# A top-k attention with a highway layer behind it: layer rows turned by DMA, one reduce for maximum and threshold, and a new order of evacuations

## The chip, the cores and the metric

The kernel runs on one core of a Trainium2 chip. The metric is the device time of one execution in microseconds. Before the change the median of three runs is 821.52 us.

## The reference, cut to what matters

Eight batch items, eight heads, 576 positions, 64 dimensions a head. Each query keeps its 32 largest scores; the result of the attention goes through a highway layer of width 512.

```python
scores = scale * np.matmul(q, k.transpose(0, 1, 3, 2))         # (8, 8, 576, 576)
kth = np.partition(scores, -32, axis=-1)[..., -32:-31]
scores = np.where(scores >= kth, scores, -1000000000.0)
attn = np.exp(scores - scores.max(-1, keepdims=True))
attn = attn / (attn.sum(-1, keepdims=True) + 1e-09)
x = np.matmul(attn, v)               # heads side by side: (4608, 512)
H = np.maximum(x @ w_h, 0.0)
T = 1.0 / (1.0 + np.exp(-(x @ w_t + b_t)))
out = T * H + (1.0 - T) * x
```

## The kernel before

**Tiling.** The 576 positions of an item are four blocks of 128 queries and a rest of 64. A unit is 128 query rows by 576 keys: one head of a full block, or two heads of the rest. Two units make a pair; an item has 18 pairs (16 of full blocks, then two of last rows), the whole kernel 144. The order is written out by hand: `step(i)` issues the instructions of several pairs in different stages, and each engine takes its own in that order. `finish` holds the last pair and the tail. A branch at the end recomputes everything if a count says that the selection was not certain; it is not taken here.

**One step.** TensorE computes the scores of pair i+2 in fp32 into PSUM (`scores`, lines 293 and 302; for last rows lines 310 and 319, where 64x64 quarters of the array are used). Two such score tiles exist, so those of pair i+2 need the place of pair i. VectorE takes the eight largest of each of six segments of a row (line 337), and from these `refine` works out a threshold near rank 24 (lines 351 to 367). `row_max` (line 372) reduces the candidates to the row's maximum. ScalarE copies the scores to SBUF (line 332), counts and marks those above the threshold (`mask_count`, line 381), and takes the exponential (line 400). TensorE adds the marks to the scores in PSUM (line 394), so that the eight largest of the rest (`below`, line 404) hold the wanted rank. `hits`, `pick_a` (GpSimd, line 420) and `pick_b` (line 423) pick it by the count. A pair later ScalarE (line 427) and GpSimd (line 438) mark the kept scores, VectorE multiplies or takes the minimum (`keep_min`, `keep_mul`, lines 434 and 444), and a DMA on SyncE's queue turns the kept rows (line 465). Three pairs later TensorE multiplies with V (`values`, line 478), whose 65th column is one, so that the sum comes along. ScalarE copies four heads of sums at a time from `pso` (line 492), that is every other step. `spare` (line 262) issues matmuls whose result nobody reads.

**Layer.** When a block of 128 rows has all heads, `ffn_pieces` makes `norm` (two small VectorE operations on the sums, lines 541 and 542, the scaling on GpSimd, line 547) and three pieces: `xt` (four transposes on TensorE, line 560, evacuated by ScalarE, line 564), `hh` and `tt` (projections, evacuated at lines 575 and 597). A step takes one piece from `layers`; its matmuls stand behind the scores of pair i+2, its evacuation is put in `late` and issued early in the next step. The rest of the layer's arithmetic is on GpSimd, in `pool_work`, and an accumulating DMA on GpSimd's queue (line 658).

**Next item.** `loads_kq` and `loads_v` bring K, Q and V. `prep_piece` turns K and Q on TensorE (line 239) and ScalarE evacuates them (line 240; line 251 to 253 for the last rows, in one piece). `prep_filler` takes such a piece in the middle of a step, beside whatever piece of a layer the step has. `todo_kq` is filled at an item's first step, `to_prep` at its seventh.

Of the kernel before, what the change touches and what calls it, by code (L numbers as in the profile page):

```python
# [10 lines left out]
ALU = mybir.AluOpType  # L11
# [6 lines left out]
J = 4  # L18
# [8 lines left out]
def kernel(  # L27
# [70 lines left out]
    wall = consts.tile([P, NU, NPK], FP32)  # L98
    fac = consts.tile([P, 4], FP32)
    nc.vector.memset(fac[:, 0:2], -scale)  # L100
    nc.vector.memset(fac[:, 2:4], -BIGK * (1.0 - 2.0**-24))
    tk = consts.tile([P, NG + 1, 4], FP32)
    be = consts.tile([P, NG + 1, 4], FP32)
# [7 lines left out]
    nc.vector.memset(tk[:, 0, 2:4], 0.0)  # L111
    nc.vector.memset(tk[:, NG, 0:2], 0.0)

    def top(u):
        return tk[:, u // 2, u % 2 : u % 2 + 1]

    def kth(u):
        return tk[:, u // 2 + 1, 2 + u % 2 : 3 + u % 2]

    def tb(u):  # L120
        return be[:, u // 2, u % 2 : u % 2 + 1]

    def eb(u):
        return be[:, u // 2 + 1, 2 + u % 2 : 3 + u % 2]

    NM = 4
# [20 lines left out]
    kds = []  # L147
    for i in range(2):
        kd = consts.tile([P, NP, P], FP32, name=f"kd{i}")
        nc.gpsimd.memset(kd[:], 0.0)  # L150
        kds.append(kd)

# [19 lines left out]
    def loads_v(b, vb):  # L172
# [11 lines left out]
        return [partial(head, h) for h in range(H)] + [partial(ends, o) for o in (0, P2)]  # L184
# [40 lines left out]

    def prep_piece(stage, prep, hp, part, ps=None, eng=None):
        kT, qT, kd = prep
# [8 lines left out]
        if part != 2:  # L236
# [3 lines left out]
            return lambda: copy(dst[:, hp, c0 * P : c1 * P], ps[:, c0 * P : c1 * P])  # L240
        for i, src in enumerate((kin, qin)):
            for h in range(NP):
# [7 lines left out]
        def evac():  # L250
            nc.scalar.copy(kd[0:D, :, 0:rem], view[0:D, 0, :, :])
            copy(kd[D:P, :, rem : 2 * rem], view[D:P, 0, :, :])
            nc.scalar.copy(qT[:, :, MAIN:S], view[:, 1, :, :])
# [17 lines left out]
    def prep_alloc(kd):  # L271
        kT = kqpool.tile([P, NP, MAIN], FP32, name="kT")
        qT = kqpool.tile([P, NP, S], FP32, name="qT")
        return kT, qT, kd
# [5 lines left out]
    def scores(pair, prep):  # L280
        kT, qT, kd = prep
# [23 lines left out]
        else:  # L305
            for (mo, ro), hh in zip(((0, RA), (MB, RB)), heads2):
                hp = hh[0] // 2
                for n0 in range(0, MAIN, 256):
                    for r in (0, D):
                        nc.tensor.matmul(  # L310
                            ps[r : r + rem, mo + n0 : mo + n0 + 256],
                            qT[r : r + D, hp, qs : qs + rem],
                            kT[r : r + D, hp, n0 : n0 + 256],
                            start=(n0 == 0),
                            stop=True,
                            skip_group_check=True,
                        )
                for r in (0, D):
                    nc.tensor.matmul(  # L319
                        ps[r : r + rem, ro : ro + rem],  # L320
                        qT[r : r + D, hp, qs : qs + rem],
                        kd[r : r + D, hp, r : r + rem],
                        start=(mo == 0),
                        stop=True,
# [17 lines left out]
    def refine(g, cand):  # L342
        u0, u1 = pairs[g][0], pairs[g][1] + 1
        en = ends[g % NE]
        runs = cand[:].rearrange("p s (k t) r -> p (s k) t r", t=2)
        one, two = runs[:, :, 0, :], runs[:, :, 1, ::-1]
# [3 lines left out]
        mid = cpool.tile([P, 2, 8], FP32, name="mid")  # L350
        nc.vector.tensor_tensor(high[:].rearrange("p (k r) -> p k r", r=8), one, two, ALU.max)  # L351
        yield
        nc.vector.tensor_tensor(low[:].rearrange("p (k r) -> p k r", r=8), one, two, ALU.min)
# [734 lines left out]
```

## Time and profile before

| | |
|---|---|
| median of 3 runs | 821.52 us (821.15 to 821.84) |
| profiled execution | 822.81 us, span 821.2 us |
| TensorE matmul, weight load | 714.2 us (87%), 517.6 us (63%) |
| VectorE | 784.9 us (96%) |
| ScalarE | 772.7 us (94%) |
| GpSimd | 556.1 us (68%) |
| mean DMA rate | 112 GB/s |

PE is TensorE's matmuls and PEld its weight loads, DVE is VectorE, ACT ScalarE, POOL GpSimd, SP SyncE. In a group of instructions the columns are the line, the engine, the operation, output and inputs, shapes and count, then the busy time in us and the mean of one in ns, and the idle time of the engine before them with what ended it. In a view of stretches the columns are the stretch and its length, the busy time of PE, PEld, DVE, ACT and POOL with instruction counts, TensorE's granted clock, the DMA share and the rate. A line of the timeline is start, duration, engine, line, operation, and in brackets the idle time before it. An fp32 matmul shows as two records.

### The profile page before, as it was taken

What the parts mean: (1) busy time and instruction counts of PE and PEld (TensorE: products, weight loads), DVE (VectorE), ACT (ScalarE), POOL (GpSimd) and SP (SyncE); (2) the same over time, 40 slices, a digit from 0 to 9 for tenths busy, and PEclk for the clock granted to TensorE, in tenths of its full rate; (3) what the DMA queues carried; (4) which work ended last, traced back from release to release, by engine and by line L of the source; (5) the groups of instructions that cost most, each with busy time, mean ns of one, the idle gap of its engine ahead of it and who ended that gap; (6) DMA issues with size and microseconds to landing.
All of it is one profiled execution on the core that took longest, in us unless ns stands there. A gap on an engine that the chain in (4) does not pass through costs nothing.

```text
span 821.2 us, 21236 instructions
## 1 busy us (share of the span) xinstructions
PE 714.2 (87%) x6687; PEld 517.6 (63%) x6687; DVE 784.9 (96%) x4162; ACT 772.7 (94%) x1438; POOL 556.1 (68%) x703
## 2 busy tenths in 40 slices
PE   7888988898889988889898898888988898888884
PEld 5666666666666666666666666666666666666552
DVE  6999999999999999999999999999999999999985
ACT  5999999999999999999999999999999999999983
POOL 2666777776677776777667776777667767666550
PEclk9999999999999999999999999999999999999998
DMA  6698878885568655775567765777556865444462
GB/s 120 84 137 140 109 105 129 140 118 84 107 126 142 108 91 110 131 137 108 83 121 132 137 104 72 133 139 131 92 94 129 142 113 97 92 88 72 103 90 74
DMA packets 323145, 91.61 MB, mean 112 GB/s; under 512 B 312144, under 2 KB 315216, under 8 KB 323024
## 3 DMA queue, kind: packets, MB, share of 16 engines
q1 hardware_dynamic: 272688, 74.76, 46.3%
q0 software_dynamic: 48656, 14.95, 18.5%
q8 instruction: 55, 0.90, 0.5%
q10 hardware_dynamic: 1680, 0.46, 0.3%
q14 instruction: 66, 0.54, 0.2%
HBM read 31.72 MB, written 9.44 MB: 50 GB/s over the span
## 4 chain that ended last, share of the span: by engine, by line
DVE 43%; ACT 39%; PE 13%; issue 2%; DMA 1%; SPq 0%; DVEq 0%; ACTq 0%
DVE cand L337 16%; DVE wall L404 12%; ACT m L381 11%; ACT e L400 8%; ACT sc L332 7%; ACT r L427 5%; PE xs L310 4%; PE pso L262 3%; DVE ep L434 3%; DVE ep L444 2%; ACT kT L240 2%; PE xs L293 1%; ACT xs L492 1%; ACT qT L240 1%; DVE en L358 1%
## 5 line engine op out<-in xcount | busy, mean ns | idle before, releaser
L337 DVE MAX8 cand<-xs 128x8 f32<-128x96 f32 x1728 | 297.4, 249 | 13.9 <-PE xs L319 9.4
L262 PE MATMUL pso<-cst,ident_b 128*128 128x252 bf16 x1935 | 256.5, 272 | 38.8 <-ACT xs L492 36.7
L438 POOL TENSOR_SCALAR ro<-sc,tk 128x576 bf16<-128x576 f32 x136 | 234.8, 1726 | 0.0
L262 PEld LDWEIGHTS <-ident_b 128*128 128x128 bf16 x1935 | 183.4, 98 | 77.8 <-issue 45.9
L400 ACT ACTIVATE e<-sc,be 128x576 bf16<-128x576 f32 x288 | 228.6, 794 | 0.0
L404 DVE MAX8 wall<-xs 128x8 f32<-128x576 f32 x288 | 204.3, 751 | 4.2 <-PE xs L394 3.6
L293 PE MATMUL xs<-kT,qT 64*128 64x256 f32 x1024 | 145.6, 400 | 35.2 <-DVE high L351 28.8
L332 ACT COPY sc<-xs 128x1152 f32<-128x1152 f32 x144 | 162.1, 1126 | 1.5 <-DVE cand L337 1.3
L293 PEld LDWEIGHTS xs<-kT,qT 64*128 64x128 f32 x1024 | 93.6, 186 | 64.7 <-issue 32.4
L381 ACT ACTIVATE m<-xs,wall 128x576 int8<-128x576 f32 x144 | 108.5, 754 | 13.1 <-DVE wall L367 10.7
L420 POOL TENSOR_TENSOR hit<-hit,wall 128x18 f32<-128x18 f32 x143 | 32.1, 225 | 128.4 <-DVE hit L410 119.1
L394 PE MATMUL xs<-m,ident_b 128*128 128x512 bf16 (+1 forms) x576 | 104.2, 285 | 11.9 <-ACT m L381 9.2
L381 ACT ACTIVATE m<-sc,wall 128x576 int8<-128x576 f32 x144 | 113.0, 784 | 0.0
L427 ACT ACTIVATE r<-sc,be 128x576 bf16<-128x576 f32 x143 | 111.4, 779 | 0.0
L375 POOL TENSOR_TENSOR be<-tk,fac 128x4 f32<-128x4 f32 x144 | 28.9, 201 | 93.4 <-DVE ep L444 51.8
L478 PEld LDWEIGHTS <-et 128*128 128x128 bf16 (+1 forms) x1600 | 68.6, 100 | 21.0 <-issue 3.5
L478 PE MATMUL pso<-vb,et 128*128 128x65 bf16 (+1 forms) x1600 | 74.6, 194 | 1.7 <-DMA et<-ep 1.6
L394 PEld LDWEIGHTS <-ident_b 128*128 128x128 bf16 x576 | 50.7, 97 | 39.7 <-issue 18.3
L302 PEld LDWEIGHTS xs<-kd,qT 128*128 128x128 f32 x256 | 38.1, 188 | 42.5 <-issue 42.1
L434 DVE TENSOR_TENSOR ep<-e,r 128x576 bf16<-128x576 bf16 x143 | 64.6, 452 | 0.1
L302 PE MATMUL xs<-kd,qT 128*128 128x128 f32 x256 | 62.5, 326 | 0.0
L444 DVE TENSOR_TENSOR ep<-e,ro 128x576 bf16<-128x576 bf16 x136 | 61.4, 452 | 0.0
(130 smaller groups left out, 1107.7 us busy)
## 6 DMA issues: line engine op xcount, KB each, us to landing
kin<-in_k_dram SPq DMA_DIRECT2D x64, 128.0 KB, 2.9
qin<-in_q_dram SPq DMA_DIRECT2D x62, 128.0 KB, 3.0
out_dram<-s SPq DMA_DIRECT2D x30, 256.0 KB, 2.5
s<-h POOLq DMA_DIRECT2D x29, 256.0 KB, 4.1
vb<-in_v_dram POOLq DMA_DIRECT2D x80, 64.0 KB, 3.2
et<-ep SPq DMA_TRANSPOSE x286, 2.7
kin<-in_k_dram SPq DMA_DIRECT2D x16, 64.0 KB, 2.4
qin<-in_q_dram SPq DMA_DIRECT2D x14, 64.0 KB, 2.5
```

The lines of the kernel that those rows point to most:

```text
L262: nc.tensor.matmul(po["t"][:, 4 * DE : BANK], ident_b[:], cst[:, 0 : BANK - 4 * DE], start=True, stop=True, skip_group_check=True,)
L293: nc.tensor.matmul(ps[:, mo + n0 : mo + n0 + 256], qT[r : r + D, hp, qs : qs + P], kT[r : r + D, hp, n0 : n0 + 256], start=(n0 == 0), stop ...
L302: nc.tensor.matmul(ends, qT[:, hp, qs : qs + P], kd[:, hp, :], start=True, stop=True)
L332: nc.scalar.copy(sc[:], both)
L337: nc.vector.max(cand[:, s, :], sc[:, s * SEG : (s + 1) * SEG])
L381: nc.scalar.activation(m1[:].bitcast(I8)[:, 1 : 2 * S : 2], ps, AF.Sign, bias=wall[:, u, 0:1], scale=ABOVE, accum_out=csum[:, u : u + 1],)
L394: nc.tensor.matmul(ps[:, s0:s1], ident_b[:], m1[:, s0:s1], start=False, stop=True, skip_group_check=True)
L400: nc.scalar.activation(e[:], sc, AF.Exp, bias=tb(u), scale=scale)
L404: nc.vector.max(wall[:, u, 1:NPK], ps)
L427: nc.scalar.activation(r[:], sc, AF.Relu, bias=eb(u), scale=BIGK)
L438: nc.gpsimd.tensor_scalar(r[:], sc, kth(u), None, ALU.is_ge)
L478: nc.tensor.matmul(pso[r0 : r0 + ql, col : col + DE], ets[s][:, c, gi * P2 : gi * P2 + ql], vb[:, h, vc, :], start=(c == 0), stop=(c == nc ...
```

## The change

- **Row maximum with threshold.** The four candidate tiles become constants with eight segment slots, of which two are filled with a very small number. `refine` writes its eight middle values into column 1 of the candidates, beside the segments' maxima in column 0, and one reduce gives the row maximum and the threshold. `row_max` goes; maxima, thresholds and picked ranks live together in `wall`.
- **Order on VectorE.** `pick_b` comes two operations earlier; the first kept row is computed between the middle values and the reduce.
- **Normaliser.** V's extra column is 2, and each head's product with V begins with an fp32 matmul of a single row that adds 2e-9, so that the reciprocal is taken directly and line 541 goes.
- **Layer rows by DMA.** For all blocks but the last three, `xt` is replaced by a cast to bf16 (a DMA on GpSimd's queue) and, two steps later, a DMA transpose on SyncE's queue; at most two such turns are under way.
- **One evacuated piece a step.** From the second item on, a step takes a piece of a layer or one of the next item's K and Q, in turn; the middle of a step takes another only where the count of pieces left asks for it. The last rows' piece is split in two (7 for K, 8 for Q).
- **Loads.** K and Q of the next item are requested two pairs sooner, their pieces become due five steps sooner; V of items after the first comes in four column loads instead of eight by head.
- **Last rows' queries as diagonal blocks.** Q of the last rows is kept in `qd` with zeros beside it, as K already was in `kd`, and the scores use the whole array with one matmul where there were two on quarters.

```diff
+    TOP, THR, KTH = 0, 1, NPK + 1
+    wall = consts.tile([P, NU + 2, NPK + 2], FP32)
...
-        nc.gpsimd.memset(vb[:, :, :, D:DE], 1.0)
+        nc.gpsimd.memset(vb[:, :, :, D:DE], 2.0)
...
+    tiny = consts.tile([1, DE], FP32)
+    nc.vector.memset(tiny[:], 0.0)
+    nc.vector.memset(tiny[:, D:DE], 2.0e-9)
+    row1 = consts.tile([1, P], FP32)
+    nc.vector.memset(row1[:], 1.0)
...
+        def column(j):
+            nc.gpsimd.dma_start(
+                vb[:, :, j, 0:D],
+                v[b, :, 0 : J * P, :].rearrange("h (p j) d -> p h j d", j=J)[:, :, j, :],
+            )
...
-            nc.scalar.copy(kd[0:D, :, 0:rem], view[0:D, 0, :, :])
-            copy(kd[D:P, :, rem : 2 * rem], view[D:P, 0, :, :])
-            nc.scalar.copy(qT[:, :, MAIN:S], view[:, 1, :, :])
+            if 0 in which:
+                nc.scalar.copy(kd[0:D, :, 0:rem], view[0:D, 0, :, :])
+                copy(kd[D:P, :, rem : 2 * rem], view[D:P, 0, :, :])
+            if 1 in which:
+                nc.scalar.copy(qd[0:D, :, 0:rem], view[0:D, 1, :, :])
+                copy(qd[D:P, :, rem : 2 * rem], view[D:P, 1, :, :])
...
-                    for r in (0, D):
-                        nc.tensor.matmul(
-                            ps[r : r + rem, mo + n0 : mo + n0 + 256],
-                            qT[r : r + D, hp, qs : qs + rem],
-                            kT[r : r + D, hp, n0 : n0 + 256],
...
+                    nc.tensor.matmul(
+                        ps[:, mo + n0 : mo + n0 + 256],
+                        qd[:, hp, :],
+                        kT[:, hp, n0 : n0 + 256],
...
                 for r in (0, D):
                     nc.tensor.matmul(
-                        ps[r : r + rem, ro : ro + rem],
-                        qT[r : r + D, hp, qs : qs + rem],
-                        kd[r : r + D, hp, r : r + rem],
+                        ps[:, ro : ro + rem],
+                        qd[:, hp, :],
+                        kd[:, hp, r : r + rem],
...
         nc.vector.scalar_tensor_tensor(
-            out=mid[:], in0=en[:, 1, :, 0:8], scalar=-1.0, in1=en[:, 0, :, 0:8], op0=ALU.mult, op1=ALU.min
+            out=cand[:, :, :, 1], in0=en[:, 1, :, 0:8], scalar=-1.0, in1=en[:, 0, :, 0:8], op0=ALU.mult, op1=ALU.min
         )
         yield
-        nc.vector.tensor_reduce(wall[:, u0:u1, 0], mid[:], mybir.AxisListType.X, ALU.max)
+        nc.vector.tensor_reduce(
+            wall[:, u0:u1, TOP : THR + 1],
+            cand[:, :, :, 0:2].rearrange("p s r k -> p s k r"),
+            mybir.AxisListType.X,
+            ALU.max,
+        )
...
-    def row_max(g):
-        nc.vector.tensor_reduce(tk[:, g, 0:2], st[g]["cand"][:, :, :, 0], mybir.AxisListType.X, ALU.max)
...
+                nc.tensor.matmul(
+                    pso[r0 : r0 + ql, col : col + DE], row1[:, 0:ql], tiny[:], start=True, stop=False
+                )
...
-            nc.vector.tensor_scalar(rinv[:, 0:nh], xs3[:, :, D], 1e-9, 2.0, ALU.add, ALU.mult)
-            nc.vector.reciprocal(rinv[:, 0:nh], rinv[:, 0:nh])
+            nc.vector.reciprocal(rinv[:, 0:nh], xs3[:, :, D])
...
-                ready.extend([xt, hh, tt])
+                if by_dma:
+                    casts.append(cast)
+                else:
+                    ready.extend([xt, hh, tt])
...
+        def cast():
+            xb = xpool.tile([P, dm], BF16, name="xb")
+            nc.gpsimd.dma_start(xb[:, 0:w], st["x"][:, 0:w])
+            return partial(turn, xb)
+
+        def turn(xb):
+            st["xT"] = fpool.tile([P, n_g, P], BF16, name="xT")
+            nc.sync.dma_start_transpose(st["xT"][:, 0:ng, :], xb[:, 0:w])
+            flying.append(b)
+            ready.extend([hh, tt])
...
+        if i == 3 or nb < B and i >= (nb - 2) * SPB + 16 > 16 - 1 and not to_prep:
+            stages[nb] = stage_tiles()
+            todo_kq.extend(loads_kq(nb, *stages[nb]))
...
-        ev = prep_filler()
+        ev = prep_filler() if to_prep and (i <= SPB or (len(to_prep) > 15 - k_in or len(layers) > 2) and i % 2) else None
...
-        if layers:
+        if layers and (last_steps or i <= SPB or kind[0] or not to_prep):
+            kind[0] = False
             late.append(layers.pop(0)())
+        elif i > SPB:
+            kind[0] = True
+            piece = prep_filler()
+            if piece:
+                late.append(piece)
...
         for _ in range(5):
             next(ra, None)
-        if nxt:
-            row_max(i + 1)
-        next(ra, None)
         if live:
             pick_b(pr, hit)
+        next(ra, None)
+        masked(0)
         for _ in ra:
             pass
...
+        last = masked(1)
...
+        while turns and turns[0][0] <= i and len(flying) < 2:
+            turns.pop(0)[1]()
```

More of the change, by code (lines that the diff above doesn't have):

```diff
@@ L182, in ends @@
             )
-        return [partial(head, h) for h in range(H)] + [partial(ends, o) for o in (0, P2)]
+        def column(j):
[3 more added lines that the diff above has]
+            )
+        mains = [partial(column, j) for j in range(J)] if b else [partial(head, h) for h in range(H)]
+        return mains + [partial(ends, o) for o in (0, P2)]
     def stage_tiles():
@@ L344, in refine @@
         en = ends[g % NE]
-        runs = cand[:].rearrange("p s (k t) r -> p (s k) t r", t=2)
-        one, two = runs[:, :, 0, :], runs[:, :, 1, ::-1]
+        one = cand[:, :, 0:NSEG:2, :]
+        two = cand[:, :, 1:NSEG:2, ::-1]
         high = cpool.tile([P, 2 * HALF], FP32, name="high")
@@ L384, in mask_count @@
             AF.Sign,
-            bias=wall[:, u, 0:1],
+            bias=wall[:, u, THR : THR + 1],
             scale=ABOVE,
@@ L731 @@
     late = []
+    kind = [False]
     def masks_of(g):
```

141 lines of the change are left out of this document (75 added, 66 removed).

## The prediction

> **What bounds the kernel now.** I read first the busy shares, then one period of the kernel (the 18 steps of one batch item) and some single steps in the view of stretches, then the groups by line, and last the timeline of single steps.
>
> ```profile
> PE 714.2 (87%) x6687; PEld 517.6 (63%) x6687; DVE 784.9 (96%) x4162; ACT 772.7 (94%) x1438; POOL 556.1 (68%) x703
> ```
>
> ```profile
> core 0: us, PE busy (x) PEld busy (x) DVE busy (x) ACT busy (x) POOL busy (x), PEclk, DMA share, GB/s
> 293.49:392.09 98.60, 87.80 (x827) 63.71 (x828) 96.31 (x515) 96.04 (x180) 71.06 (x89) 1.00 0.66 116
> ```
>
> ```profile
> 299.25:304.48 5.23, 4.77 (x42) 3.15 (x42) 5.23 (x28) 4.61 (x9) 3.91 (x4) 1.00 0.46 72
> 352.42:358.13 5.71, 4.67 (x47) 3.33 (x47) 5.32 (x29) 5.62 (x13) 4.52 (x8) 1.00 0.80 139
> 358.13:363.89 5.76, 5.17 (x51) 3.70 (x52) 5.33 (x28) 5.76 (x12) 3.90 (x4) 1.00 0.90 128
> 385.59:392.09 6.50, 5.81 (x60) 4.05 (x59) 5.61 (x32) 6.50 (x14) 5.24 (x7) 1.00 0.68 118
> ```
>
> The first rows show two engines full at once: a period of 98.60 us holds 96.31 of DVE and 96.04 of ACT. The steps show that they take turns. In the first step DVE never rests (5.23 of 5.23) and ACT has 0.62 us over. In the next two ACT has 13 and 12 instructions instead of 9, because a piece of a layer and a piece of the next item's K or Q are both evacuated in that step; DVE idles 0.39 and 0.43 us there. The last one, where the last rows' pairs begin, has both and loses 0.89 us on DVE. So a period is DVE's work plus some 2.3 us in which DVE waits for an overloaded ACT, or for PE at the last rows. Relief on DVE alone would soon run into ACT, and the change relieves both. PE is not far behind, and what the change puts on it is my main doubt.
>
> **DVE: the row maximum and the sum's small operation.**
>
> ```profile
> L372 DVE TENSOR_REDUCE tk<-cand 128x2 f32<-128x12 f32 x144 | 22.3, 155 | 0.0
> L337 DVE MAX8 cand<-xs 128x8 f32<-128x96 f32 x1728 | 297.4, 249 | 13.9 <-PE xs L319 9.4 <-PE xs L302 4.4
> L404 DVE MAX8 wall<-xs 128x8 f32<-128x576 f32 x288 | 204.3, 751 | 4.2 <-PE xs L394 3.6 <-PE pso L478 0.2
> L541 DVE TENSOR_SCALAR rinv<-xs 128x8 f32<-128x8 f32 (+1 forms) x38 | 6.3, 165 | 0.0
> ```
>
> ```profile
> 407.20 0.16 DVE L372 TENSOR_REDUCE tk<-cand 128x2 f32<-128x12 f32 x1
> 407.31 0.17 DVE L363 SCALAR_TENSOR_TENSOR mid<-en 128x16 f32<-128x16 f32 x1
> ```
>
> ```profile
> 424.29 0.17 DVE L541 TENSOR_SCALAR rinv<-xs 128x4 f32<-128x4 f32 x1
> 424.49 0.18 DVE L542 RECIPROCAL rinv<-rinv 128x4 f32<-128x4 f32 x1
> ```
>
> Small operations overlap at their ends, so a removed one is worth its distance to the next start. The row maximum starts 0.11 us before its successor. The reduce that takes it over reads 16 elements more; an element costs (751-249)/480 = 1.05 ns between the two MAX8 rows, hence 0.02. That leaves 0.09 x 18 steps = 1.6 us a period. The removed add-and-double holds the reciprocal off by 0.20 us, five times a period (40 blocks in 8 periods): 1.0. Together -2.6, bounded by -0.5 (if the strided writes into the candidates cost as much as they save) and -3.6 (at the full 155 and 165 ns).
>
> The threshold now comes after the first kept row (0.45 us later, less what was removed), so ACT's masks may start later; ACT is the engine that lags in most steps, so I cost that at nothing. If ACT stood waiting there, it would be 0.3 us a step. The sum of the hits now follows the four small MAX8 directly; its input comes from POOL, which must be prompt:
>
> ```profile
> POOL hit L420 <- DVE hit L410: 119.1, 137, 3.6
> ```
>
> POOL waits 0.87 us for it in the mean, so it is there early. The casts (five DMA issues a period, price below) stand behind that operation, and the V loads go from eight issues to four, so POOL stays near its 71 of 98.6 us.
>
> **ACT: the turned layer rows and the pieces.**
>
> ```profile
> L564 ACT CAST xT<-fp 128x512 bf16<-128x512 f32 (+1 forms) x37 | 20.4, 552 | 0.0
> L251 ACT COPY kd<-fp 64x256 f32<-64x256 f32 x7 | 2.6, 369 | 0.4
> L658 POOL DMA_DIRECT2D s<-h x36 | 33.3, 925 | 8.2 <-POOL hit L420 8.2
> ```
>
> All 37 of these casts go to DMA: 5 x 0.55 = 2.75 us a period. The last rows' queries take two quarter copies instead of one half: +0.37. ACT falls from 96.04 to about 93.7, just over DVE's 93.7 (96.31-2.6), so neither is left far above the other. With one piece a step the collisions of the second and third step above should go: -0.8. I leave the 0.89 of the fourth step in, since PE is late there as well.
>
> **PE: diagonal blocks for the last rows.**
>
> ```profile
> 290.73 0.60 PE L239 MATMUL fp<-ident_f,qin 128*128 128x128 f32 x4
> 291.26 1.08 PE L310 MATMUL xs<-kT,qT 64*64 64x256 f32 x8
> 292.18 0.28 PE L319 MATMUL xs<-kd,qT 64*64 64x64 f32 x4
> 292.29 1.03 PE L310 MATMUL xs<-kT,qT 64*64 64x256 f32 x8
> ```
>
> ```profile
> DVE cand L337 <- PE xs L319: 9.4, 16, 0.9
> ```
>
> Eight 256-column records take 0.92 us on 64x64 quarters, 0.115 each. If those are pairs that run side by side in two quarters, four whole-array records at 0.23 take the same 0.92. The four 64-column records of a head pair now take 0.11; as whole-array records each needs a 128-column fp32 weight load. The nearest row is the transposes, four in 0.53, 0.133 each. That is +0.42 a half, +0.84 a pair, at most 1.7 a period; if the loads hide behind the wider records it is half of that or less. DVE already waits in all 16 such pairs, 0.59 us in the mean, so nothing covers it. I take +1.2 a period; the lower bound is -1.2 (the wait of 2 x 0.59 goes), the upper +1.7.
>
> **PE: a start matmul for every head.** Each of 40 heads a period gets one fp32 matmul of one row by 65 columns, two records.
>
> ```profile
> 299.15 1.04 PE L506 MATMUL fp<-wh,xT 128*128 128x512 bf16 x4
> 300.02 0.59 PE L262 MATMUL pso<-cst,ident_b 128*128 128x252 bf16 x4
> 300.45 0.65 PE L394 MATMUL xs<-m,ident_b 128*128 128x512 bf16 x4
> 300.94 0.48 PE L478 MATMUL pso<-vb,et 128*128 128x65 bf16 x10
> 301.88 1.02 PE L262 MATMUL pso<-cst,ident_b 128*128 128x252 bf16 x8 [0.46 <-ACT xs L492]
> 302.83 1.14 PE L293 MATMUL xs<-kT,qT 64*128 64x256 f32 x8
> 303.90 0.49 PE L302 MATMUL xs<-kd,qT 128*128 128x128 f32 x2
> 304.22 1.03 PE L506 MATMUL fp<-wt,xT 128*128 128x512 bf16 x4
> ```
>
> ```profile
> 406.67 1.13 PE L293 MATMUL xs<-kT,qT 64*128 64x256 f32 x8 [0.51 <-DVE high L351]
> ```
>
> With 0.133 a record (the transposes again: the same weight load, twice the columns) it is 0.27 a head, 0.53 a step of two heads. Ends: 0.03 a record as the quarter records above (0.11 a step), and 0.163 as L302 (two in 0.32), 0.65 a step. The Trainium skill ("TensorE: Matmul & The Clock Gate", section "LDWEIGHTS (loading the stationary operand)") says that a weight load goes by its columns and not by its rows, P/1.2 ns, so the single row is no saving. By that, two loads of 128 columns, an estimate, are 0.21 a head and 0.43 a step, a little under my row; no one-row load of 128 columns is in the trace.
>
> In a step without the copy of sums, PE stands 0.51 us before it may overwrite the scores: this hides the 0.53. In a step with that copy PE's own loop is 5.07 us from one late piece to the next (299.15 to 304.22) and waits only for ACT's copy, which itself waits for the values. There 0.53 counts. With a projection as the late piece the loop becomes 5.60; with four transposes (0.53 instead of 0.87) it is 5.26, below the pace of 5.4 that comes out here. Pieces alternate and copies alternate: out of phase it costs nothing, in phase 9 x 0.25 = 2.3. I take +0.6. The dropped transposes of layer rows were a late piece too, so they save nothing in the loop beyond that.
>
> **DMA: the layer rows.**
>
> ```profile
> 390.62 2.52 SPq L465 DMA_TRANSPOSE et<-ep  x2
> DMA to landing us min/median/max: 2.4/2.7/6.5
> ```
>
> The turn is issued behind a step's two transposes (2.52 us of SP) and lands about 2.5 later, some 5.0 us after the first kept row is ready; the projection that reads it stands behind the next step's scores, about a step and 0.4 us after. A margin near 0.7 us: nothing in the sum. The cast has two steps. Earlier loads and their SP issues fall into gaps of SP; nothing.
>
> **The sum.** A period: -2.6 -0.8 +1.2 +0.6 = -1.6, so 98.6 becomes 97.0, eight times: -12.8. The tail, where start matmuls of the last four pairs lie on PE's path and one DVE operation of 0.17 goes twice: +1. The profiled execution took 822.81 (span 821.2), so 811.0; the median of the shown runs is 1.29 lower: 809.7. I say 810.
>
> **Rivals.**
>
> *The relief arrives whole.* The last rows cost nothing more and the phases of pieces and copies lie apart: -3.4 a period, -27, so 795. For it: ACT and DVE floors are both 93.7. Against: 128-column fp32 loads in a place where DVE waits already.
>
> *PE becomes the bound (slower).* Place: PE's in-order loop. Half the steps have the 5.07 loop, half 4.61 without the wait of 0.46: 4.84. Of 18 late pieces some eight become transposes (-0.34 each) and five carry the bias matmul (+0.22): 4.75. Start matmuls at L302's price: 0.65; last rows 1.7/18 = 0.09. That is 5.49 a step without any wait for DVE, 98.8 a period; with 0.1 us a step left of the wait of 0.51, 100.6: +2.0 x 8 + 1, so 838. It decides from about 0.16 us a record on. At 0.133 the same loop is 5.37, 96.7. By the Trainium skill's rule above, the loop would be 5.27; that speaks against this rival.
>
> *The turned rows land late.* If landings take 1.3 us more than the median, the margin is gone and the projection holds PE for 0.6 us, and with it masks and scores: 37 x 0.6 = 22, so 832; if only in one block of three, 817. For: single landings up to 6.5, and DMA shares of 0.80 and 0.90 in the steps above. Against: the median.
>
> *The smoothing does not do what it says.* Pieces fall due at the item's end and two are still taken in a step: -0.8 is lost, 816.
>
> **How the numbers follow.** 0.2% is about what a measurement of this kernel can tell from no change. Forecast 0.50 (797 to 818), whole relief 0.13, PE the bound 0.17, late rows 0.13, no smoothing 0.07. Faster: 0.50+0.13+0.06, and 0.02 of PE, 0.03 of late rows: 0.74. Same: 0.02 of PE, 0.03 of late rows, 0.01 of no smoothing: 0.06. Slower: 0.13+0.07 = 0.20. The range 790 to 828 takes in the ends of the last rows and of the start matmuls, and leaves out the worse half of PE (838), of late rows (832) and the lowest of the whole relief.
>
> **What would show it.** The reduce of both maxima at about 190 ns, no row maximum; DVE busy about 764; ACT about 755 with no cast from the transposes; steps with 0.4 us of idle DVE in the middle of a period gone; DVE's wait for the last rows' tail over 9.4 us, towards 19. I am wrong if start matmuls take over 0.16 us a record, if PE waits for DMA ahead of the projections by over 5 us in total, or if ACT waits long for the threshold.

## The result and the profile after

| | us | against before, 95% interval |
|---|---|---|
| before | 821.35 (821.15 to 821.84) | |
| after | 900.69 (899.73 to 902.05) | 1.0966 (1.0947 to 1.0985) |

The change makes the kernel 79 us slower. The forecast was 810 in a range of 790 to 828; the result lies above the range, and above the slower rival's 838 as well.

The page of after, first the busy shares (PE, PEld, DVE, ACT, POOL), then the shares of the chain that ended last:

```profile
PE 843.6 (94%) x7011; PEld 606.5 (67%) x7011; DVE 777.2 (86%) x3984; ACT 766.3 (85%) x1408; POOL 559.2 (62%) x714
...
PE 78%; ACT 15%; DVE 5%; DMA 1%; issue 1%; SPq 0%; ACTq 0%; DVEq 0%
```

TensorE has become the bound: 843.6 us of work where there were 714.2, and 78% of the chain. VectorE and ScalarE did fall (784.9 to 777.2, 772.7 to 766.3), but now they wait. The groups by line and the waits of after say where the work is and who waits for it:

```profile
L499 PE MATMUL pso<-tiny,row 1*128 1x65 f32 (+1 forms) x640 | 131.4, 285 | 0.0
L504 PE MATMUL pso<-vb,et 128*128 128x65 bf16 (+1 forms) x1600 | 107.5, 198 | 0.0
```

```profile
ACT xs L518 <- PE pso L504: 72.2, 72, 2.5
DVE cand L360 <- PE xs L326: 71.9, 106, 3.2
...
DVE cand L360 <- PE xs L342: 25.7, 16, 2.1
ACT m L404 <- DVE wall L389: 16.5, 44, 1.0
```

The wait of the copy of sums in before, for comparison:

```profile
ACT xs L492 <- PE pso L478: 9.8, 28, 0.6
```

Line 499 is the start matmul of each head: 640 records that were not there before. Line 504 is the products with V, the same 1600 records as before. ScalarE's copy of sums waits 72.2 us for those products, where it waited 9.8, and VectorE's first maximum 71.9 us for the scores, where it waited 4.4 (the row of L337 in the prediction). The threshold wait of the masks, 16.5 us where it was 10.7, is small beside them.

The price of a start is read in the timeline from one fixed piece of work to the next. From the start of four mask matmuls over the ten products of two heads to the spare matmuls, before and after:

```profile
392.89 0.65 PE L394 MATMUL xs<-m,ident_b 128*128 128x512 bf16 x4
393.38 0.48 PE L478 MATMUL pso<-vb,et 128*128 128x65 bf16 x10
393.70 1.02 PE L262 MATMUL pso<-cst,ident_b 128*128 128x252 bf16 x8
```

```profile
414.89 0.65 PE L417 MATMUL xs<-m,ident_b 128*128 128x512 bf16 x4
415.47 0.43 PE L499 MATMUL pso<-tiny,row 1*128 1x65 f32 x2
415.83 0.33 PE L504 MATMUL pso<-vb,et 128*128 128x65 bf16 x5
416.09 0.43 PE L499 MATMUL pso<-tiny,row 1*128 1x65 f32 x2
416.46 0.33 PE L504 MATMUL pso<-vb,et 128*128 128x65 bf16 x5
416.63 1.02 PE L286 MATMUL pso<-cst,ident_b 128*128 128x252 bf16 x8
```

393.70 - 392.89 = 0.81 us became 416.63 - 414.89 = 1.74: two starts add 0.93 us to a step, 0.46 a head. The time is in more places than the starts' own. The first start begins 0.58 after the masks instead of 0.49; each takes 0.36 to the first product; and the first head's five products take 0.26 to the next start, where half of ten products before is 0.16. So the stream loses some 0.1 us each time that it turns to a start, and the rest of the 0.93 lies between a start and its first product. A period of 18 steps went from 98.60 to 108.78:

```profile
317.87:426.65 108.78, 103.69 (x861) 74.51 (x860) 94.91 (x491) 95.24 (x177) 71.20 (x89) 0.98 0.72 115
```

PE is busy 103.69 us of it. With 0.93 x 18 = 16.7 us less it would be at 87, as before (87.80).

### The profile page after: what moved, and what is told of

It reads as the page before. It is cut to its first block, busy times and chain, and to the rows that moved or that the text cites. A ratio compares the mean times of both kernels' runs of the same rounds, so it can differ in the third digit from the quotient of the medians.

```text
span 899.1 us, 21764 instructions
## 1 busy us (share of the span) xinstructions
PE 843.6 (94%) x7011; PEld 606.5 (67%) x7011; DVE 777.2 (86%) x3984; ACT 766.3 (85%) x1408; POOL 559.2 (62%) x714
## 4 chain that ended last, share of the span: by engine, by line
PE 78%; ACT 15%; DVE 5%; DMA 1%; issue 1%; SPq 0%; ACTq 0%; DVEq 0%
PE pso L286 19%; PE xs L317 12%; PE pso L499 11%; PE pso L504 9%; PE xs L417 7%; PE fp L532 6%; ACT m L404 5%; PE xs L326 4%; PE xs L333 3%; ACT e L423 3%; ACT xs L518 3%; ACT sc L355 2%; PE fp L257 2%; DVE cand L360 2%; PE xs L342 1%; DVE wall L427 1%
## 5 line engine op out<-in xcount | busy, mean ns | idle before, releaser
L360 DVE MAX8 cand<-xs 128x8 f32<-128x96 f32 x1728 | 299.0, 249 | 99.3 <-PE xs L326 71.9
L286 PE MATMUL pso<-cst,ident_b 128*128 128x252 bf16 x1881 | 252.9, 273 | 34.6 <-ACT xs L518 32.5
L461 POOL TENSOR_SCALAR ro<-sc,wall 128x576 bf16<-128x576 f32 x135 | 232.5, 1722 | 0.0
L286 PEld LDWEIGHTS <-ident_b 128*128 128x128 bf16 x1881 | 177.9, 98 | 74.4 <-issue 41.6
L423 ACT ACTIVATE e<-sc,be 128x576 bf16<-128x576 f32 x288 | 225.0, 781 | 0.2
L317 PE MATMUL xs<-kT,qT 64*128 64x256 f32 x1024 | 149.1, 410 | 2.5 <-ACT qT L258 1.5
L499 PE MATMUL pso<-tiny,row 1*128 1x65 f32 (+1 forms) x640 | 131.4, 285 | 0.0
L404 ACT ACTIVATE m<-xs,wall 128x576 int8<-128x576 f32 x144 | 106.7, 741 | 16.7 <-DVE wall L389 16.5
L499 PEld LDWEIGHTS pso<-tiny,row 1*128 1x128 f32 (+1 forms) x640 | 86.9, 172 | 43.2 <-issue 34.0
L504 PE MATMUL pso<-vb,et 128*128 128x65 bf16 (+1 forms) x1600 | 107.5, 198 | 0.0
L518 ACT COPY xs<-pso 128x260 f32<-128x260 f32 x72 | 27.0, 375 | 72.2 <-PE pso L504 72.2
L398 POOL TENSOR_TENSOR be<-wall,fac 128x4 f32<-128x4 f32 x144 | 28.5, 198 | 71.1 <-DVE ep L467 53.6
L417 PEld LDWEIGHTS <-ident_b 128*128 128x128 bf16 x576 | 50.6, 98 | 32.5 <-issue 10.2
```

What stands on the lines that cost most here:

```text
L286: nc.tensor.matmul(po["t"][:, 4 * DE : BANK], ident_b[:], cst[:, 0 : BANK - 4 * DE], start=True, stop=True, skip_group_check=True,)
L317: nc.tensor.matmul(ps[:, mo + n0 : mo + n0 + 256], qT[r : r + D, hp, qs : qs + P], kT[r : r + D, hp, n0 : n0 + 256], start=(n0 == 0), stop ...
L360: nc.vector.max(cand[:, s, :], sc[:, s * SEG : (s + 1) * SEG])
L404: nc.scalar.activation(m1[:].bitcast(I8)[:, 1 : 2 * S : 2], ps, AF.Sign, bias=wall[:, u, THR : THR + 1], scale=ABOVE, accum_out=csum[:, u ...
L417: nc.tensor.matmul(ps[:, s0:s1], ident_b[:], m1[:, s0:s1], start=False, stop=True, skip_group_check=True)
L423: nc.scalar.activation(e[:], sc, AF.Exp, bias=tb(u), scale=scale)
```

## The experiments

**The start matmuls alone, from both sides.** First the change without them, and the kernel before with them and nothing else of the change.

```diff
 # a1_no_start, against after
-                nc.tensor.matmul(
-                    pso[r0 : r0 + ql, col : col + DE], row1[:, 0:ql], tiny[:], start=True, stop=False
-                )
...
-                        start=False,
+                        start=(c == 0),
```

> The changed kernel without the start matmul of each head (the 2e-9 is left out; the first product with V starts the sum). Theory S, the start matmuls filled TensorE: in the changed profile a head's start and its five products take 0.62 us from start to start where five products alone took 0.16, so 0.46 x 320 heads = 147 us of TensorE go; a period of 18 steps falls from 108.8 to 96 to 98 and the time to 798 to 812. Theory R, the other parts (diagonal blocks, turned rows, the new order) carry a good part of the loss: the time stays over 830, and TensorE's or VectorE's idle time moves to them.

> The kernel before, with nothing new but the fp32 one-row start matmul of each head (1e-9, and the sum's small operation doubles only). Theory S: TensorE's loop of about 4.75 us a step grows by 0.92 and becomes the pace; a period goes from 98.6 to 104 to 110, the time to 865 to 905. Theory R: the start matmuls find room beside the waits of TensorE, under 840.

Without the starts the changed kernel takes 828.19 us, 1.0074 of before (1.0053 to 1.0096); with them the kernel before takes 912.93, 1.1119 (1.1100 to 1.1137). So they cost 72.5 us in the one and 91.6 in the other, and account for nearly all of the result. The first run falls between the two ranges that were expected of it, the second above both. What is left is smaller and just as unforeseen: the forecast's sum without its +0.6 is 2.2 us a period faster, and without the starts the change is 7 us in all slower.

**What makes a start dear.** It differs from the products behind it in two things, its type (fp32, two records) and its single row. Each was changed alone and both together, and one run shares a single start among all the heads of a pair.

```diff
 # a3_start_bf16: both; c2_start_bf16_row: the type alone; c3_start_fp32_full: the rows alone
-    tiny = consts.tile([1, DE], FP32)
+    tiny = consts.tile([P, DE], BF16)        # a3
+    tiny = consts.tile([1, DE], BF16)        # c2
+    tiny = consts.tile([P, DE], FP32)        # c3
 # a4_one_start
+                if s == 0 and gi == 0:
+                    nh = 2 * len(heads)
...
+                        tiny[:, 0:nh, :],
```

> The changed kernel with the start matmul in bf16 over 128 rows (the constant tile of 1/256 against 4e-9), as many instructions as before less the second fp32 record. Theory S in the form that the price is the change between fp32 and bf16 and the drain at it: a start costs about as much as a product with V, 0.03 to 0.05 us, and the time is within 6 us of the kernel without starts. In the form that any matmul between two heads costs it (a new weight load and a new sum): over 860. Theory R: as the changed kernel without starts, over 830.

> The changed kernel with one fp32 one-row start matmul for all heads of a pair (130 or 260 columns) instead of one for each head: 144 instead of 320. Theory S: each change from bf16 to fp32 and back costs some 0.4 us, so a step of two heads keeps about 0.5 of its 0.92; the time is about halfway, 820 to 850. If the price went by columns and not by changes, it would stay over 880. Theory R: over 870.

> The changed kernel with the start matmul in bf16, still of one row. If the price is the change of type between fp32 and bf16: a start costs as in a3_start_bf16, 825 to 830. If it is the single row, that is the change of the array's row group: near the changed kernel's 900, less the second record, 860 to 890.

> The changed kernel with the start matmul in fp32 over 128 rows (1/256 against 4e-9). If the price is the type: as the changed kernel, 890 to 905. If it is the single row: the price falls to two weight loads of some 0.11 each, 0.27 a head instead of 0.46, 840 to 860.

| start | us | masks to spare matmuls, two heads |
|---|---|---|
| none (a1) | 828.19 | 0.81 (before) |
| bf16, 128 rows (a3) | 826.94 | 0.87 |
| fp32, 128 rows (c3) | 841.12 | 1.23 |
| bf16, one row (c2) | 850.60 | 1.28 |
| fp32, one row (after) | 900.69 | 1.74 |
| fp32, one row, once a pair (a4) | 849.59 | 1.33 |

The last column is read as above, from these rows of the timelines of a3, c2 and c3 (in a4 from 405.41 to 406.74):

```profile
404.33 0.44 PE L415 MATMUL xs<-m,ident_b 128*128 128x512 bf16 x3
404.82 0.19 PE L497 MATMUL pso<-tiny,cst 128*128 128x65 bf16 x1
404.85 0.32 PE L502 MATMUL pso<-vb,et 128*128 128x65 bf16 x5
...
405.20 1.02 PE L284 MATMUL pso<-cst,ident_b 128*128 128x252 bf16 x8
```

```profile
404.36 0.65 PE L417 MATMUL xs<-m,ident_b 128*128 128x512 bf16 x4
404.94 0.20 PE L499 MATMUL pso<-tiny,row 1*128 1x65 bf16 x1
405.07 0.33 PE L504 MATMUL pso<-vb,et 128*128 128x65 bf16 x5
405.34 0.20 PE L499 MATMUL pso<-tiny,row 1*128 1x65 bf16 x1
...
405.64 1.02 PE L286 MATMUL pso<-cst,ident_b 128*128 128x252 bf16 x8
```

```profile
402.00 0.65 PE L417 MATMUL xs<-m,ident_b 128*128 128x512 bf16 x4
402.49 0.33 PE L499 MATMUL pso<-tiny,row 128*128 128x65 f32 x2
402.66 0.32 PE L504 MATMUL pso<-vb,et 128*128 128x65 bf16 x5
402.82 0.41 PE L499 MATMUL pso<-tiny,row 128*128 128x65 f32 x2
...
403.23 1.02 PE L286 MATMUL pso<-cst,ident_b 128*128 128x252 bf16 x8
```

A start of the products' own type and rows takes 0.03 us (404.82 to 404.85), like any further product. In bf16 with one row it takes 0.13 (404.94 to 405.07), and the products before the next one take 0.27 instead of 0.16: the change of rows costs some 0.1 us in each direction. In fp32 over 128 rows two records take 0.17, and 0.25 where the start follows the first head's products (402.82 to 403.07, where the next products begin). Against a3's 0.87, the type alone adds 0.36 a step, the row alone 0.41, and both together 0.87, a little more than their sum.

What the single row changes can be seen in the weight loads. These are the loads of a start in a3 and in c2, and of a start and the products behind it in after:

```profile
404.61 0.10 PEld L497 LDWEIGHTS <-cst 128*128 128x128 bf16 x1
```

```profile
404.94 0.09 PEld L499 LDWEIGHTS <-row 1*128 1x128 bf16 x1 [0.24 <-issue]
```

```profile
403.64 0.29 PEld L499 LDWEIGHTS pso<-tiny,row 1*128 1x128 f32 x2 [0.24 <-issue]
404.00 0.21 PEld L504 LDWEIGHTS <-et 128*128 128x128 bf16 x5
```

Over 128 rows the load begins 0.21 us ahead of its matmul (404.61 for 404.82), beside the matmuls before it. With one row it begins only with its matmul (404.94 in c2; 403.64 in after, where the matmul starts at 403.65), and so does the load of the first product behind it (404.00 for 404.01). The load itself is no longer for it: 0.09 us with one row, 0.10 with 128. A load of 0.1 us that nothing covers is about the 0.1 us of a turn; that it is the whole of it is a reading of these rows, and no run separates it.

The times follow the prices only in part. Against a1's 828.19, c3, c2 and a4 cost 13, 22 and 21 us, by 144 steps 0.09, 0.16 and 0.15 of their 0.42, 0.47 and 0.52 (against 0.81). So TensorE seems to have room for the first 0.3 to 0.4 us of a step. Of what comes on top, about three quarters goes into the time (0.93 - 0.47 = 0.46 us by 144 steps is 66, and 50 were measured). That is why c2 lies between its two expected ranges: neither the type nor the row alone makes the price.

**The 7 us without starts.** All the following leave the start matmuls out, and so the 1e-9 of the sum, except where the text says otherwise. Two candidates showed in the trace of a1. One is a place in ScalarE's queue: the evacuation of a projection's result into `h`, of which there are two buffers, and the accumulating DMA that reads `h` (line 697). The timeline of a1, its waits, and the stretch of that step:

```profile
607.42 0.93 POOL L697 DMA_DIRECT2D s<-h  x1 [0.26 <-POOL hit L443]
...
613.54 0.60 ACT L613 ACTIVATE h<-fp 128x512 f32<-128x512 f32 x1 [3.25 <-PE xs L326]
```

```profile
ACT h L613 <- DMA s<-h: 3.7, 3, 1.4
ACT h L613 <- PE xs L326: 3.3, 1, 3.3
```

```profile
613.53:624.27 10.74, 7.14 (x50) 4.85 (x52) 5.77 (x29) 10.43 (x19) 5.88 (x8) 0.76 0.64 100
```

The DMA issued at 607.42 lands 6.0 us later, at about 613.4, and the evacuation starts at 613.54. The row names a matmul that ended at 613.49, but that matmul has nothing to do with `h`; I read the DMA as the releaser, and the run with four buffers tests it. ScalarE stands 3.25 us, and with it everything behind; the step that follows takes 10.74 us instead of some 5.4, and TensorE's granted clock falls to 0.76 in it. The period with this step takes 105.2 us in a1's trace, the six before it 97.2 to 98.8. The other candidate is the last rows' scores, in the timelines of before and after, one pair:

```profile
293.16 0.28 PE L319 MATMUL xs<-kd,qT 64*64 64x64 f32 x4
293.37 0.66 PE L560 MATMUL fp<-ident_f,x 128*128 128x128 f32 x4
```

```profile
423.88 1.03 PE L333 MATMUL xs<-kT,qd 128*128 128x256 f32 x4
424.75 0.56 PE L342 MATMUL xs<-kd,qd 128*128 128x64 f32 x4
425.14 1.08 PE L333 MATMUL xs<-kT,qd 128*128 128x256 f32 x4
426.06 0.56 PE L342 MATMUL xs<-kd,qd 128*128 128x64 f32 x4
426.45 1.03 PE L532 MATMUL fp<-wh,xT 128*128 128x512 bf16 x4
```

Before, the pair took 293.37 - 291.26 = 2.11 us (its first rows are in the prediction), after 426.45 - 423.88 = 2.57. The four records of 64 columns now take 0.39, where they took 0.11 to 0.21.

```diff
 # b1_h_buffers, against a1
+    hpool = ctx.enter_context(tc.tile_pool(name="hp", bufs=4))
-            h2 = fpool.tile([P, dm], FP32, name="h2")
+            h2 = hpool.tile([P, dm], FP32, name="h2")
 # b2_quarters, against a1: the scores and the copy of the last rows' queries as before the change
-                        qd[:, hp, :],
+                            qT[r : r + D, hp, qs : qs + rem],
 # b3_vector_only, against a1: also layer rows by PE and ACT, pieces in the old order
-        by_dma = isinstance(b, int) and units[-1][0:2] > (b, qt + 2)
+        by_dma = False
```

> The changed kernel without start matmuls (as a1_no_start, which took 828.2), and four buffers instead of two for the tile h of the layer. Theory H: the rare long steps of a1_no_start (one of 10.7 us, some of 6.5 to 8) come from ScalarE standing at the evacuation of a projection until the accumulating DMA of a block two before has read its h; projections follow each other sooner now that the transposes are no piece of their own. Then ScalarE's wait there (3.7 us on the DMA, 3.3 beside it) goes with what hangs on it: 820 to 824. Theory X: the long steps come from turned rows that land late; TensorE's wait for them (4.5 us in a1_no_start) stays and the time stays over 826.

> As a1_no_start, with the last rows' scores on 64x64 quarters again (and the last rows' queries evacuated in one copy). Theory Q: a pair of last rows takes 2.57 us as diagonal blocks in the changed profile against 2.11 before, and VectorE's wait for its tail is 17.8 us against 9.4; 16 x 0.46 = 7.4, so 820 to 823. Rival: TensorE is late there for other reasons and the blocks are hidden, no change from 828.

> As a1_no_start, but with the layer rows turned by TensorE and ScalarE again, two pieces a step as before, the pieces due at the seventh step and quarters for the last rows: what is left of the change is the maximum with the threshold, the order on VectorE, the reciprocal without the small operation, and the earlier loads. Theory V: VectorE's 0.09 us a step and 1.0 a period show only where VectorE sets the pace; ScalarE still carries 96.0 of 98.6 us a period, so about half shows: 808 to 814. If the later threshold holds ScalarE: over 819.

> As a1_no_start with both: four buffers for h and quarters for the last rows. If H and Q both hold and add up, 813 to 817, under the kernel before; if only one holds, 820 to 824; if neither, 826 or more.

| | us | against before |
|---|---|---|
| b1, four buffers | 820.62 | 0.9985 (0.9973 to 0.9997) |
| b2, quarters | 817.47 | 0.9948 (0.9934 to 0.9962) |
| b4, both | 812.28 | 0.9896 (0.9881 to 0.9911) |
| b3, VectorE's part and the sooner loads alone | 820.44 | 0.9989 (0.9980 to 0.9998) |

The buffers are worth 7.6 us, the quarters (with the single copy of the queries) 10.7, both 15.9. In b1 no wait of the evacuation on the accumulating DMA is left, while TensorE still waits for turned rows (5.7 us where a1 has 4.5), so theory X is out. VectorE's part alone gains 0.9 us, about a twentieth of what the prediction gave it and far from the 808 to 814 that were expected. The time does lie in the range of the other theory, that the later threshold holds ScalarE; but that wait is 13.7 us in b3 against 10.7 before, too little for the 6 us and more by which the theory was missed. Its period and its first maximum:

```profile
582.53:681.13 98.60, 87.54 (x815) 64.03 (x826) 94.72 (x492) 96.24 (x181) 67.89 (x84) 1.00 0.70 116
```

```profile
L360 DVE MAX8 cand<-xs 128x8 f32<-128x96 f32 x1728 | 298.5, 249 | 25.6 <-PE xs L342 13.0 <-PE xs L325 12.2
```

The period is 98.60 as before. VectorE works 1.6 us less in it (94.72 against 96.31) and waits that much more for the scores (25.6 against 13.9 us in all), while ScalarE still has 96.24.

**VectorE's part where ScalarE has been relieved.** c1 puts its two removed operations back into b4: a second reduce a step and a small operation ahead of the reciprocal.

```diff
 # c1_vector_put_back, against b4
-            nc.vector.reciprocal(rinv[:, 0:nh], xs3[:, :, D])
+            nc.vector.tensor_scalar(rinv[:, 0:nh], xs3[:, :, D], 0.0, 1.0, ALU.add, ALU.mult)
+            nc.vector.reciprocal(rinv[:, 0:nh], rinv[:, 0:nh])
...
+            nc.vector.tensor_reduce(
+                cond[:, 0:2], st[i + 1]["cand"][:, :, 0:NSEG, 0], mybir.AxisListType.X, ALU.max
+            )
```

> As b4_buffers_quarters (812.3), with VectorE's cost put back: a second reduce for the row maximum at its old place, whose result nobody reads, and the small operation ahead of the reciprocal. Theory B (both reliefs are needed): b3 with VectorE's relief alone gained 0.9 us, because ScalarE's collisions set those steps; with ScalarE relieved, VectorE sets the pace in most steps and its 0.1 us a step and 1.0 a period come to 18 to 22, of which part shows: 820 to 830. Rival: ScalarE's relief alone makes the gain of b4, 811 to 815.

It takes 813.90, 0.9915 (0.9900 to 0.9929): 1.6 us more than b4, by intervals that overlap, and in the range of the rival. One period of b4 and of c1:

```profile
573.68:669.78 96.10, 83.41 (x780) 60.01 (x791) 94.47 (x492) 93.80 (x175) 71.33 (x89) 1.00 0.79 132
```

```profile
576.25:673.02 96.77, 83.47 (x781) 60.03 (x792) 95.26 (x516) 93.96 (x175) 71.33 (x89) 1.00 0.76 131
```

This pair differs by 0.67 us. Over the first seven periods of the two traces c1 takes 3.0 us more, 0.4 a period, and single periods differ by -0.4 to +1.3. So the two operations cost 0.2 to 0.4 us a period here, which is not clear of the noise; the 820 to 830 of theory B is refuted.

**Which of ScalarE's two edits gains.** b4 still takes layer rows by DMA and one evacuation a step. d3 keeps the DMA and goes back to the old order, in which the middle of a step takes a piece whenever there is one, the pieces fall due at the seventh step and the last rows' piece is whole. The loads stay two pairs sooner, other than its expectation says.

```diff
 # d3_two_pieces, against b4
-        ev = prep_filler() if to_prep and (i <= SPB or (len(to_prep) > 15 - k_in or len(layers) > 2) and i % 2) else None
+        ev = prep_filler()
-            if k_in == (1 if b else 7):
+            if k_in == (6 if b else 7):
...
-        if layers and (last_steps or i <= SPB or kind[0] or not to_prep):
+        if layers:
```

> b4_buffers_quarters with the order of before for the pieces: ScalarE evacuates up to two pieces a step, the turned queries of the last rows are one piece, loads of two pairs are not sooner. The layer rows still go through DMA, VectorE's part stays, four buffers, quarters, no start (the 1e-9 to 2e-9 of the sum is left out). Theory A (the order of one piece a step carries the gain beyond the vector part, since collisions of ACT pieces cost 8 x 0.8 us by the prediction): 812.3 + 6.4 = 818.7, 817 to 821. Theory B (taking 4 evacuations a block off ScalarE by DMA carries it, the order is worth under 0.2 us a period): 811 to 814.

It takes 821.25, 1.0000 (0.9991 to 1.0009): the order with its sooner due pieces is worth 9.0 us, near theory A, and without it nothing is gained. Two steps in which both kinds of piece fell due in d3, the same two of b4, and the period of d3:

```profile
650.67:656.50 5.83, 5.30 (x51) 3.73 (x51) 5.31 (x28) 5.74 (x13) 4.32 (x8) 1.00 1.09 152
656.50:662.17 5.67, 5.08 (x49) 3.61 (x49) 5.24 (x27) 5.67 (x12) 3.91 (x4) 1.00 0.79 124
...
602.17:701.33 99.16, 89.47 (x840) 64.84 (x839) 94.96 (x493) 94.01 (x175) 71.23 (x90) 1.00 0.79 127
```

```profile
638.22:643.57 5.35, 4.29 (x40) 3.10 (x40) 5.23 (x29) 5.35 (x11) 3.89 (x7) 1.00 0.83 144
643.57:648.80 5.23, 4.72 (x43) 3.32 (x42) 5.23 (x27) 4.97 (x10) 4.32 (x5) 1.00 0.75 129
```

ScalarE has 13 and 12 instructions and sets the pace in the first two, 11 and 10 in the last two. Over the period both kernels have the same work on VectorE (94.96 and 94.47) and on ScalarE (94.01 and 93.80), and they differ by 3 us (over seven periods of the traces by 2.0 a period, and by the medians by 1.1): what matters here is less how much ScalarE has than how it is spread. That the layer rows by DMA bring nothing by themselves isn't shown by this, since in d3 the late turned rows (next) hold TensorE for 8.2 us.

**The turned rows.** In b4 TensorE waits for them ahead of the projections:

```profile
PE fp L530 <- DMA xT<-xb: 5.7, 6, 2.3
```

A second row, at line 540, has 2.0 us more.

c4 and d1 put a turned block's two projections on the list of layer pieces one step later. In c4 some pieces of the last turned block were never issued, so it leaves out a part of one block's layer; in d1 all are. d2 is d1 with the starts of a3, so that it has the whole of the computation.

```diff
 # c4_late_projection and d1_late_projection_whole, against b4
-            ready.extend([hh, tt])
+            soon.extend([hh, tt])
...
         layers.extend(ready)
         ready.clear()
+        ready.extend(soon)                                  # c4
+        (layers if last_steps else ready).extend(soon)      # d1
+        soon.clear()
```

> As b4_buffers_quarters (812.3), with the projections of a turned block offered one step later. In b4 TensorE waits 6.5 us for turned rows, in steps that last 6 to 8.2 us instead of 5.2. If landings late by a part of a step are the whole of it, these steps go to 5.2: 804 to 809. If the delay moves projections onto other crowded steps instead: 811 to 815.

> Like c4_late_projection (the two projections of a turned block are put on the list of layer pieces one step after the transposing transfer), but the pieces of the last turned block are not held back in the last eight steps, so that all of them are issued. Without the start matmuls, so the 1e-9 to 2e-9 in the sum of the softmax is left out. Theory (TensorE's 6.5 us of waiting for turned rows in b4_buffers_quarters is all that the later projection removes): 812.3 - 5 = 807, 806 to 808.5, since the last block's few pieces cost at most what one layer piece costs a step, 0.1 to 0.3 us. Rival (c4's gain came in part from the pieces that it never issued): 809 to 812.

> d1_late_projection_whole plus the start matmul in bfloat16 over all 128 rows, one a head as in the change, so that the sum of the softmax has its 2e-9 again: the whole of the change, with four buffers for the layer tile and 64 x 64 quarters for the last rows' scores. Theory (a start of the products' own type and rows costs TensorE about 0.03 us a record, and TensorE is not the bound): within 2 us of d1, 805 to 809. Rival (in a kernel with fewer stalls TensorE's 640 added records lie on the path): 640 x 0.03 / 2 = 10 us and more above d1, 815 to 825.

c4 takes 807.17, d1 807.45 (0.9836, 0.9822 to 0.9849), d2 809.29 (0.9854, 0.9839 to 0.9869). TensorE's wait for turned rows is not among the waits of d1 any more, and 4.8 of its 7.7 us came out of the time. One period takes 96.81 us in d1 and 97.03 in d2.

d2 beats before by 12 us with the whole computation: the change with its start over 128 rows in bf16, four buffers for `h`, the last rows on quarters, and the projections a step later.

## Why the prediction was wrong

**The step that failed: "0.133 a record", "I take +0.6".** The start matmuls cost 72.5 us, 9.1 a period where +0.6 was in the sum. The mechanism was named, as the slower rival with a chance of 0.17, and the size was wrong twice. First the price: fp32 transposes standing four in a row gave 0.133 a record, 0.53 a step; a start alone between products of another type and of more rows gave 0.93. What was missing is the neighbours: no row of before shows an fp32 or one-row matmul singly between bf16 ones, and the upper end, 0.163 from L302, was read behind the turn and not over it. The bound from above was therefore not one. The trace of before did show a turn between row counts: at line 302 matmuls over 128 rows follow others over 64, and the weight loads stand idle ahead of theirs, 0.33 us each of 127 times. What that costs was not measured.

```profile
PEld xs L302 <- issue: 42.1, 127, 0.3
```

Second the conversion: of the 18 x 0.53 = 9.5 us a period that its own price gives, the prediction let 0.6 count, since the 0.51 us where TensorE waits for VectorE would hide the starts of one step and alternating pieces those of the next. With a price below that, 0.47 a step, c2 already cost 22 us, 2.8 a period. The rival's own loop with the measured price is 4.75 + 0.93 + 0.09 + 0.1 = 5.87 us a step, 105.7 a period, and some 58 us in all; 79 were measured, with a period of 108.8. The decision point was put too high as well: 0.16 us a record is 0.65 a step, and c3 and c2, at 0.42 and 0.47, cost 13 and 22 us against a1.

The Trainium skill ("TensorE: Matmul & The Clock Gate", section "LDWEIGHTS (loading the stationary operand)") has the load's time go by columns and not by rows, by which 0.43 a step was estimated and which was held against the rival. For the load itself the traces agree (0.09 us with one row in c2, 0.10 with 128 in a3). But with the same 128 columns, one row in place of 128 cost 0.41 us a step in bf16 (1.28 against 0.87) and 0.51 in fp32 (1.74 against 1.23). The rule is for a load by itself; what decided here is the turn from one row count to another, at which the load no longer runs ahead (404.94 in c2). The estimate left it out.

**Last rows on diagonal blocks, +1.2 a period: right.** One pair takes 0.46 us more, and going back gains 10.7 us, 1.3 a period, or 8.3 us, 1.0 a period, where `h` has four buffers. VectorE's wait for their tail was to rise from 9.4 towards 19: 25.7 in after, 17.8 in a1, 9.0 in b4.

**VectorE, -2.6 a period: too large, and hidden.** The merged reduce took 204 ns, not 190, and the operation that writes the middle values 189 ns instead of 175 (the strided write that only the lower bound had). VectorE fell by 12.3 us in b3 (784.9 to 772.6), 1.5 a period, not 2.6. Of that nothing reached the period while ScalarE kept its collisions, and when they were gone c1's two operations, which give back 0.8 us of work a period, cost 0.2 to 0.4. The prediction had seen that the two engines take turns, and still put the relief into the sum as if each paid out by itself. The later threshold, put at nothing, lengthened ScalarE's wait for it from 10.7 us to 16.5 in after and 20.6 in d1; what that costs was not measured.

**One evacuation a step, -0.8: right, and larger.** 9.0 us, 1.1 a period; the steps of 5.7 to 5.8 became 5.2 to 5.35. The rival in which the smoothing fails does not hold.

**Layer rows by DMA, 0 with a margin of 0.7 us: a partial miss.** The late rows cost 4.8 us, 0.6 a period, about a fifth of the 22 that this rival gave them, and the sign that was named (over 5 us of waiting ahead of the projections) appeared in a1: 4.5 and 1.8 us in two rows. The removed casts took ScalarE to 757.7 in d1 (755 forecast).

**Not foreseen at all: the two buffers of `h`.** The evacuation of a projection meets a buffer that a DMA of 6.0 us still reads: 7.6 us. The kernel before has the same two buffers and no such wait in its trace. That a block's projections run closer together with `xt` gone is a likely reason, and was not shown. The prediction had followed each queue and each moved transfer, but not the buffers that the pieces share.

With the starts in bf16 over 128 rows, the quarters, the buffers and the later projections, the kernel takes 809.3; that this is near the forecast of 810 is chance, since the forecast's terms were not these.

**Open.** The sooner loads and the column loads of V were never taken out alone, and the new order was never run without the layer rows by DMA. Why b1 and b2 together gain 2.4 us less than their sum was not pursued. What after loses beyond the rival's loop, some 20 us, has no single row.

## What to carry to other kernels

A small matmul put into a stream of others is priced by its neighbours: given the type and the rows of the matmuls behind it, it cost what one more of them costs. When two engines are full and take turns, relief on one can be worth next to nothing while steps overload the other (0.9 us of 20.8 here); look at the steps, not at the sums. When pieces of work are moved closer together, look for the buffers they share, and how long the slowest transfer holds one.

## What was not expected of the hardware

One row of weights instead of 128, with the same columns, costs TensorE about 0.1 us on each turn to it and back (404.94 to 405.07 for a record of 0.03 otherwise; 0.27 instead of 0.16 for the five products ahead of the next one). At such a turn the load of the weights begins with its matmul (404.94) and not 0.21 us ahead of it (404.61 for 404.82), though it takes no longer. Two fp32 records between bf16 ones take 0.17 to 0.25 us. Both together, 0.46 us a head, added 72.5 us to 828.
